# Later weight conversions for the second layer, token factors formed step by step, and a reordered last unit

## The chip, the cores and the metric

The kernel runs on one core of a Trainium2 chip. The metric is the device time of one execution in microseconds (us). TensorE (PE) multiplies, VectorE (DVE), ScalarE (ACT) and GpSimd (POOL) do the elementwise work, and SyncE (SP) and ACT issue DMA transfers. Each engine works through its own instructions in a fixed order and waits on semaphores for the others.

## The reference

Four batches of 576 tokens pass through three blocks:

```
phi(x)  = [exp(p), exp(-p)],  p = x w_phi - max|x w_phi|
attn    = phi(q) (phi(k)^T v) / (phi(q) sum_s phi(k) + 1e-6)
x       = heads of attn side by side                        # 4 x 576 x 512
u       = x + Re(FFT over tokens and features of x)
layer 1 : u + relu(norm(u) w_ch1) w_ch2                     # 512 -> 2048 -> 512
layer 2 : u = x + (relu(x^T w_tok1) w_tok2)^T               # tokens 576 -> 256 -> 576
          u + relu(u w_ch1) w_ch2                           # 512 -> 1536 -> 512
```

The weights of both layers come as 64-bit floats.

## The kernel before

All products are made in pairs of a rounded part ("high") and what is left ("low"): three matmuls (high-high, high-low, low-high) stand for one product. A weight must first be converted from its 64-bit words. `words` and `words2` do this for a block of 128x512: a DMA of 512 KB into a tile `raw`, one ACT instruction (L510), three DVE instructions on 128x512 words (L513, L514, L516). What follows splits the result into high (a copy on ACT) and low (a subtraction on POOL).

Layer 1's weights are converted by `w_ahead` (during the attention, stored to DRAM) and `w_now` (16 blocks for its third and fourth groups of hidden features, while its first groups are multiplied). Layer 2's channel weights go through `w_seven` and `wa_seven`: 24 blocks, in which four sums and differences of sub-blocks are made on POOL (L623 to L626), seven 128x128 parts are split (L632 on ACT, L636 on POOL), and high and low are stored to DRAM by SP (L645). Each of these 24 results is half of a tile `ring` of 1792 KB that `w_load` fetches later. Nine more blocks (`wa_plain`) hold the token weights.

Layer 2's channel products use seven products in place of eight, as in Strassen's scheme in Winograd's form. One `unit` takes 256 hidden features and one batch: seven products of token factors `x` with weights (`prod`, L859), sums and ReLUs on DVE, ACT and POOL that give seven new factors `g` (`part`, splits on POOL at L895, shown in the trace as L1283), and seven products of those (`prod2`, L868), each added to `u` on DVE by `flush` (L922, or L917 in the last unit of a batch, whose result goes to a tile `t` of three buffers and from there to DRAM). There are 24 units: batches 2 and 3 by turns through six parts of the features, then batches 0 and 1. The token factors of a batch (seven tiles `x`, from four differences `xq`) are made by `x_prep`: L827 on ACT, L830 on DVE or POOL, L833 on DVE.

The order on each engine is written out by a planner: every step is put on a list with a planned time (`at`, `later`), and the list is emitted in the order of these times. A planned time sets only the order; on the chip each instruction runs when its inputs and its place are there. Pools of tiles (`cv`, `cv2`, `r`, `g` and others) have fixed numbers of buffers, and a new tile waits for the last use of the buffer that it takes. Layer 1 ends where the token step (`c_tr`, `c_tok1`, `c_tok2`) begins.

In the traced execution: attention and FFT until about 320 us, layer 1 until 725, the token step until 790, the units until the end.

Of the kernel before, what the change touches and what calls it, by code (L numbers as in the profile page):

```python
# [9 lines left out]
F32 = mybir.dt.float32  # L10
# [36 lines left out]
HB = 288  # L47
# [7 lines left out]
def mixer_kernel(ctx: ExitStack, tc: tile.TileContext, qT, kT, vt, wphi, w11, w12, wt1, wt2, w21, w22,  # L55
# [439 lines left out]
    def words(src, n, cols, then, lag=0.0, tag="t"):  # L495

        home = P["cv2" if n is None or tag == "t2" else "cv"]
        raw = home.tile([128, 512, 2], U32, tag="raw", name="raw", bufs=2)
        if n is None:
            n = 128  # L500
            nc.sync.dma_start(out=raw.rearrange("q (j c) t -> q j c t", j=2), in_=src)
        else:
            nc.sync.dma_start(out=raw[0:n, 0:cols], in_=src)
        later(lag, words2, home, raw, n, cols, then, tag)

    def words2(home, raw, n, cols, then, tag):
        lo, hi = raw[0:n, 0:cols, 0], raw[0:n, 0:cols, 1]
        t = home.tile([128, 512], U32, tag=tag, name="t", bufs=2 if tag == "t2" else 1)
        v = t[0:n, 0:cols]
# [9 lines left out]
        later(V('dT', 2.8), then, v.bitcast(F32), *((raw,) if tag == 't2' else ()))  # L519
# [69 lines left out]
    def part_tile():  # L589
        return P["cv2"].tile([128, 7, 128], F32R, tag="y", name="wst", bufs=4)  # L590

    def wa_plain(key, src, n, cols):

        def then(v, raw):
# [19 lines left out]
    def wa_seven(key, src, eng):  # L614

        _, m, which, p, s = key

        def then(v, raw):
            blk = v.rearrange("q (a c) -> q a c", a=4)
            a11, a21, a12, a22 = (blk[:, n] for n in range(4))  # L620
            x = raw.rearrange("q c t -> q (c t)").bitcast(F32)[:, 0:512].rearrange("q (a c) -> q a c", a=4)
            ve = nc.gpsimd if eng == "pool" else nc.vector
            ve.tensor_tensor(out=x[:, 0], in0=a21, in1=a22, op=ALU.add)  # L623
            ve.tensor_tensor(out=x[:, 1], in0=x[:, 0], in1=a11, op=ALU.subtract)
            ve.tensor_tensor(out=x[:, 2], in0=a11, in1=a21, op=ALU.subtract)
            ve.tensor_tensor(out=x[:, 3], in0=a12, in1=x[:, 1], op=ALU.subtract)  # L626
            parts = [(slice(0, 1), blk[:, 0:1]), (slice(1, 3), blk[:, 2:4]), (slice(3, 7), x)]
            yh, yl = part_tile(), part_tile()

            def hi():  # L630
                for o, a in parts:
                    nc.scalar.copy(out=yh[:, o], in_=a)  # L632

            def lo():
                for o, a in parts:
                    nc.gpsimd.tensor_tensor(out=yl[:, o], in0=a, in1=yh[:, o], op=ALU.subtract)  # L636
                mark("wa", key)
                store(0, yh)

            def store(h, y):  # L640
                need(("wa", key))
                mark("wd", key)
                if (m, which, p) not in WD:
                    WD[m, which, p] = dr.tile([128, 2, 2, 7, 128], F32, name=f"wd{m}{which}{p}")
                nc.sync.dma_start(out=WD[m, which, p][:, s, h], in_=y.bitcast(F32))  # L645
            later(1.9, hi)
            later(3.2, lo)
            later(5.8, store, 1, yl)
        words(src, None, 512, then, V('wl', 5.0), 't2')

    def w_seven(p, which, s, eng="pool"):
# [161 lines left out]


    XI = {1: 0, 2: 1, 3: 2, 5: 3, 7: 4, 6: 5, 4: 6}
    WI = {1: 0, 2: 1, 4: 2, 5: 3, 6: 4, 7: 5, 3: 6}

    def x_prep(b, slot):

# [6 lines left out]
        def hi(n, a):  # L826
            nc.scalar.copy(out=X[n][:, 0], in_=a)  # L827

# [513 lines left out]
```

## Time and profile before

| | |
|---|---|
| median of 3 runs | 1104.27 us (1102.8 to 1104.54) |
| the profiled execution | 1102.2 us, of which its span is 1100.2 us |
| PE busy, matmuls | 1041.6 us, 7596 |
| DVE, ACT, POOL busy | 724.3, 447.5, 457.1 us |
| mean granted clock of PE | 0.98 |

Times in the rows are from the start of the span. A row of the stages gives the length of a stretch and, for each engine, its busy time with the number of instructions. Busy time of PE says little where its matmuls are held up, so the number of matmuls in a stretch is the better measure of pace.

### The profile page before, as it was taken

Reading aid. Unit: us, or ns where it says so; the run is one execution under the profiler, and the core shown is the slowest. Engines: PE = TensorE matmul, PEld = TensorE weight load, DVE = VectorE, ACT = ScalarE, POOL = GpSimd, SP = SyncE. Lnnn points to the kernel's source line nnn. Section 1 sums busy time; section 2 is a strip of 40 time slices with the busy share of each in tenths; the row PEclk is TensorE's granted clock in tenths of the full one; section 3 lists DMA queues with packets and bytes.
Section 4 is the critical chain, followed back from the end, with each engine's and each line's share of the span. In section 5 each row is a group of like instructions: output and inputs, shape, how many; then the busy total and the mean of one; then the engine's idle time right before and its main releaser. Section 6 shows DMA issues by size and latency. Waiting matters only on the chain.

```text
span 1100.2 us, 19639 instructions
## 1 busy us (share of the span) xinstructions
PE 1041.6 (95%) x7596; PEld 959.1 (87%) x7596; DVE 724.3 (66%) x1273; ACT 447.5 (41%) x1002; POOL 457.1 (42%) x483
## 2 busy tenths in 40 slices
PE   9999999999998788999998999999999998799997
PEld 9887787868898777999998999997889997799997
DVE  5788797999757788554466434246656667666665
ACT  6766556552124443332243212124344444434442
POOL 3363434322026654463444100001156657655654
PEclk9999999999999999999998999999999998899998
DMA  5565564362358764268643255450013543454532
GB/s 182 175 214 170 164 223 160 117 225 72 121 186 277 283 230 145 103 195 310 255 162 112 81 210 197 129 202 1 1 68 142 193 142 131 156 195 141 192 139 86
DMA packets 59945, 178.41 MB, mean 162 GB/s; under 512 B 7892, under 2 KB 23188, under 8 KB 53196
## 3 DMA queue, kind: packets, MB, share of 16 engines
q1 hardware_dynamic: 48332, 99.56, 27.4%
q10 hardware_dynamic: 11520, 77.60, 18.9%
q8 instruction: 60, 0.98, 0.4%
q14 instruction: 33, 0.27, 0.1%
HBM read 126.39 MB, written 48.31 MB: 159 GB/s over the span
## 4 chain that ended last, share of the span: by engine, by line
PE 52%; DVE 7%; POOL 3%; issue 2%; DMA 2%; ACT 1%; ACTq 0%; SPq 0%; DVEq 0%; POOLq 0%
PE pw L780 13%; PE pz L868 11%; PE pw L859 10%; PE pk L802 2%; PE pk L803 2%; PE pa L802 2%; PE pk L804 2%; PE pa L804 2%; PE pa L803 2%; DMA outT<-t 1%; POOL g L1283 1%; DVE t L514 1%; DVE xq L833 1%; PE pw L1062 1%; PE pk L1043 1%
## 5 line engine op out<-in xcount | busy, mean ns | idle before, releaser
L780 PE MATMUL pw<-xh,w 128*128 128x288 f32 x896 | 198.6, 296 | 0.0
L868 PE MATMUL pz<-g,ring 128*128 128x288 f32 x1008 | 160.5, 304 | 9.3 <-POOL g L1283 5.6
L859 PE MATMUL pw<-x,ring 128*128 128x288 f32 x1008 | 152.8, 298 | 8.6 <-DVE f L881 5.0
L788 DVE SCALAR_TENSOR_TENSOR gl<-pw,gh 128x288 fp32r<-128x288 f32 x128 | 57.9, 454 | 155.0 <-ACT gh L787 154.9
L868 PEld LDWEIGHTS pz<-g,ring 128*128 128x128 f32 x1008 | 143.8, 193 | 16.0 <-POOL g L1283 11.1
L922 DVE TENSOR_TENSOR u<-u,pz 128x576 f32<-128x576 f32 x152 | 114.3, 753 | 61.8 <-PE pz L868 58.0
L780 PEld LDWEIGHTS pw<-xh,w 128*128 128x128 f32 x896 | 151.2, 189 | 1.2 <-issue 1.0
L859 PEld LDWEIGHTS pw<-x,ring 128*128 128x128 f32 x1008 | 140.5, 190 | 11.4 <-DVE f L881 6.5
L780 PE MATMUL pw<-xl,w 128*128 128x288 f32 x448 | 133.0, 297 | 0.5 <-POOL xl L763 0.5
L787 ACT ACTIVATE gh<-pw 128x288 fp32r<-128x288 f32 x128 | 52.4, 409 | 195.3 <-PE pw L780 192.7
L1283 POOL TENSOR_TENSOR g<-t,g 128x576 fp32r<-128x576 f32 x48 | 70.6, 1470 | 54.4 <-ACT g L894 51.9
L199 POOL TENSOR_TENSOR l<-raw,h 128x384 fp32r<-128x384 f32 x48 | 51.7, 1081 | 95.3 <-ACT h L195 86.7
L803 PE MATMUL pk<-gl,w 128*128 128x288 f32 x256 | 78.9, 308 | 12.0 <-DVE gl L788 11.8
L802 PE MATMUL pk<-gh,w 128*128 128x288 f32 x256 | 77.6, 303 | 11.5 <-DVE u L807 5.1
L780 PEld LDWEIGHTS pw<-xl,w 128*128 128x128 f32 x448 | 84.8, 189 | 0.7 <-POOL xl L763 0.7
L1283 POOL TENSOR_TENSOR g<-f,g 128x288 fp32r<-128x288 f32 x72 | 59.3, 837 | 50.3 <-ACT g L894 50.3
L802 PE MATMUL pa<-gh,w 128*128 128x288 f32 x256 | 77.2, 302 | 0.0
L804 PE MATMUL pk<-gh,w 128*128 128x288 f32 x256 | 77.0, 301 | 0.0
L804 PE MATMUL pa<-gh,w 128*128 128x288 f32 x256 | 76.9, 300 | 0.0
L803 PE MATMUL pa<-gl,w 128*128 128x288 f32 x256 | 76.7, 299 | 0.0
L1283 ACT ACTIVATE f<-f 128x288 f32<-128x288 f32 x72 | 32.0, 444 | 101.8 <-DVE f L881 101.7
L259 PEld LDWEIGHTS pk<-v,ek 128*128 128x128 f32 x512 | 61.6, 192 | 5.8 <-issue 5.8
(195 smaller groups left out, 2400.7 us busy)
## 6 DMA issues: line engine op xcount, KB each, us to landing
ring<-wd ACTq DMA_DIRECT2D x24, 1792.0 KB
raw<-in_w SPq DMA_DIRECT2D x56, 512.0 KB
w<-wd ACTq DMA_DIRECT2D x24, 1024.0 KB
wd<-wst SPq DMA_DIRECT2D x48, 448.0 KB
wd<-wst SPq DMA_DIRECT2D x16, 512.0 KB
wd<-w ACTq DMA_DIRECT2D x32, 256.0 KB
v<-in_v SPq DMA_DIRECT2D x8, 650.0 KB
raw<-in_k SPq DMA_DIRECT2D x24, 192.0 KB
```

Of the source, the lines that this page charges most:

```text
L199: nc.gpsimd.tensor_tensor(out=l, in0=src, in1=h, op=ALU.subtract)
L259: nc.tensor.matmul(T["kv", i][j][:, o:o + 65], e[:, (t % 2) * 2 + j, s, :], v[:, t - 1, j * 65:j * 65 + 65], start=False, stop=(u == 1 and ...
L780: nc.tensor.matmul(out, w[:, k, fs], x[:, k, :], start=(n == 0), stop=(n == 11))
L787: nc.scalar.activation(out=gh, in_=out, func=AF.Relu)
L788: nc.vector.scalar_tensor_tensor(out=gl, in0=out, scalar=0.0, in1=gh, op0=ALU.max, op1=ALU.subtract)
L802: nc.tensor.matmul(out, wh[:, f % 4, ds], gh, start=(f == f0), stop=False)
L803: nc.tensor.matmul(out, wh[:, f % 4, ds], gl, start=False, stop=False)
L804: nc.tensor.matmul(out, wl[:, f % 4, ds], gh, start=False, stop=last)
L859: nc.tensor.matmul(out, w[:, kk, hw, WI[i]], x[XI[i]][:, hx, kk], start=(start and k == 0), stop=(stop and k == 5), skip_group_check=(i != 2))
L868: nc.tensor.matmul(o[s], w[:, s, hw, WI[i]], g[hx], start=(start and k == 0), stop=(stop and k == 2), skip_group_check=(i != 2))
L922: nc.vector.tensor_tensor(out=u, in0=u, in1=o, op=ALU.add)
L1283: fn(*a, **k)
```

## The change

- `w_seven` and `wa_seven` become one function. The seven parts are laid out so that one ACT copy and one POOL subtraction of 128x896 take the place of three each; the low half is written into `raw`, which has three buffers now; the load of a block is three DMAs instead of one.
- The 33 conversions for layer 2 begin 40 planned us before the end of layer 1's first three blocks (`tb2 - 40`), and not 20 after the FFT (`zend + 20`). Six of the 24 blocks (`late`) are left out there and converted from `td - 16` on, one each 15 planned us, `td` being the start of the units. These use the pool `cv`, whose tag `raw` the token step also uses.
- `ring` is loaded by SP and not by ACT.
- `x_prep` makes each token factor by itself: a high part is put just behind the old factor's last product, its low part 1.6 us later. For batches 2 and 3 all differences and low parts go to POOL; for batches 0 and 1 the differences go to DVE, and they begin three units and one unit earlier.
- In the last unit (`end`) the second products stand earlier and in another order, four splits and one sum move from POOL to DVE, and product 2 is flushed in two halves.

```diff
     def words(src, n, cols, then, lag=0.0, tag="t"):
-        home = P["cv2" if n is None or tag == "t2" else "cv"]
-        raw = home.tile([128, 512, 2], U32, tag="raw", name="raw", bufs=2)
+        home = P["cv2" if tag == "t2" else "cv"]
+        raw = home.tile([128, 512, 2], U32, tag="raw", name="raw", bufs=3 if tag == "t2" else 2)
...
     def part_tile():
-        return P["cv2"].tile([128, 7, 128], F32R, tag="y", name="wst", bufs=4)
+        return P["cv2"].tile([128, 7, 128], F32R, tag="y", name="wst", bufs=3)
...
-    def w_seven(p, which, s, eng="pool"):
+    def w_seven(p, which, s, late=False):
...
+        home = P["cv" if late else "cv2"]
+        raw = home.tile([128, 512, 2], U32, tag="raw", name="raw", bufs=2 if late else 3)
+        for o, n, j, c in ((0, 128, 0, 0), (128, 256, 1, 0), (384, 128, 0, 128)):
+            nc.sync.dma_start(out=raw[:, o:o + n], in_=src[:, j, c:c + n])
+        L = raw.rearrange("q c t -> q (c t)").bitcast(F32)[:, 0:896]
...
+        def then(v):
+            a11, a12, a22, a21 = (v[:, n * 128:(n + 1) * 128] for n in range(4))
+            x = [N["x"][:, n * 128:(n + 1) * 128] for n in range(4)]
+            for o, a, c, op in ((0, a21, a22, ALU.add), (1, x[0], a11, ALU.subtract), (2, a11, a21, ALU.subtract),
+                                (3, a12, x[1], ALU.subtract)):
+                nc.gpsimd.tensor_tensor(out=x[o], in0=a, in1=c, op=op)
...
+            def hi():
+                for o, e, a in N["parts"]:
+                    nc.scalar.copy(out=yh[:, o:e], in_=a)
+            def lo():
+                for o, e, a in N["parts"]:
+                    nc.gpsimd.tensor_tensor(out=L[:, o:e], in0=a, in1=yh[:, o:e].bitcast(F32), op=ALU.subtract)
+                store(0, yh.bitcast(F32))
...
+            later(V('sh', 3.2), hi)
+            later(V('sl', 4.8), lo)
+            later(V('ss', 8.0), store, 1, L)
+        later(12.0 if late else V('wl', 5.0), words2, raw, room, then)
...
     def w_load(which, p, v):
-        nc.scalar.dma_start(out=t.bitcast(F32), in_=WD[1, which, p])
+        nc.sync.dma_start(out=t.bitcast(F32), in_=WD[1, which, p])
...
+    XP = {1: 2, 0: 1, 5: 6, 4: 7, 3: 5, 2: 3, 6: 4}
+    POS = {2: 0, 1: 1, 6: 4, 7: 5, 5: 8, 3: 11, 4: 13}
+    def x_prep(b, slot, td_, t0, step, engs):
...
         def diff(o, a, c):
-            nc.vector.tensor_tensor(out=o, in0=a, in1=c, op=ALU.subtract)
+            (nc.gpsimd if "d" in engs else nc.vector).tensor_tensor(out=S_[o], in0=S_[a], in1=S_[c], op=ALU.subtract)
...
+        for n, a in enumerate(((3, "12", 0), (5, 2, 3), (4, 2, "12"), (6, 1, 5))):
+            at(td_ + 0.01 + step * n, diff, *a)
+        for n, i in XP.items():
+            t = t0(POS[i])
+            at(t, hi, n)
+            at(t + 1.6, lo, n)
...
         def y2():
-            open_z("y")
-            second(2, "y", True, True, 0, 0)
+            if not end:
+                open_z("y")
+                return second(2, "y", True, True, 0, 0)
+            o = [pw()[:, 0:HB] for _ in range(2)]
+            prod2(2, o, True, True)
+            for m in range(2):
+                later(0.3, flush, o[m].unsqueeze(1), 0, 0, (m,))
...
-        for k, fn in ((20, x1), (21, z7), (23, x6), (24, z4), (26, x5), (30, y2), (31, x3)):
+        second_ = ((20, x1), (21, z7), (23, x6), (24, z4), (26, x5), (30, y2), (31, x3))
+        if end:
+            second_ = ((17.1, x1), (17.6, z7), (18.2, x6), (18.8, x5), (19.2, x3), (19.8, y2), (20.4, z4))
+        for k, fn in second_:
             at(t0 + k * st_, fn)
...
-    tcv = zend + V('c2', 20)
+    late = ahead[18:24]
+    del ahead[18:24]
+    tcv = tb2 - V('c2', 40)
     for n, (kind, *a) in enumerate(ahead):
         at(tcv, w_seven if kind == "s" else wa_plain, *a)
-        tcv += V('c3', 12) if n < 8 else V('c4', 9.3)
+        tcv += V('c4', 9.3)
...
-    at(td - 36, x_prep, 2, 0)
-    at(td - 20, x_prep, 3, 1)
-    at(times1[11] - 0.6, x_prep, 0, 0)
-    at(times1[12] - 0.6, x_prep, 1, 1)
+    x_prep(2, 0, td - 44, lambda k: td - 42.5 + 1.4 * k, 1.6, "d0123456")
+    x_prep(3, 1, td - 22, lambda k: td - 21 + 1.6 * k, 1.6, "d0123456")
+    x_prep(0, 0, times1[8], lambda k: times1[10] + (k + 8) * TU / 14, TU / 3, "016")
+    x_prep(1, 1, times1[11] + 11 * TU / 14, lambda k: times1[11] + (k + 9) * TU / 14, 0.7, "016")
+    for n, (_, p, which, s) in enumerate(late):
+        at(td - 16 + 15 * n, w_seven, p, which, s, True)
```

On POOL, in a unit of the channel products, the order before is (L902 and L909 make sums for the factors, L1283 splits them):

```order
L902 TENSOR_TENSOR t<-f 128x288
L1283 TENSOR_TENSOR g<-t,g 128x576
L909 TENSOR_TENSOR t<-f,t 128x288
L1283 TENSOR_TENSOR g<-f,g 128x288 x2
L1283 TENSOR_TENSOR g<-t,g 128x576
L1283 TENSOR_TENSOR g<-f,g 128x288
```

In the changed kernel POOL meets this in one of the first units (L919 and L926 are the old L902 and L909, L1319 the old L1283; L644 and L656 belong to a late conversion):

```order
L926 TENSOR_TENSOR t<-f,t 128x288
L1319 TENSOR_TENSOR g<-f,g 128x288 x2
L644 TENSOR_TENSOR raw<-t 128x128
L644 TENSOR_TENSOR raw<-raw,t 128x128
L644 TENSOR_TENSOR raw<-t 128x128
L644 TENSOR_TENSOR raw<-t,raw 128x128
L1319 TENSOR_TENSOR g<-t,g 128x576
L656 TENSOR_TENSOR raw<-raw,wst 128x512
L656 TENSOR_TENSOR raw<-t,wst 128x384
L1319 TENSOR_TENSOR g<-f,g 128x288
```

A block of four small instructions now stands ahead of the unit's last split of 128x576, and a block of two larger ones behind it. Six conversions bring two such blocks each; in the units their places differ.

On DVE, where the units turn from batches 2 and 3 to batches 0 and 1, the order before is (L833 makes a difference, L830 a low part of a token factor, L881 and L922 belong to units):

```order
L833 TENSOR_TENSOR xq<-u 128x576
L881 TENSOR_TENSOR f<-pw,c_10526 128x288
L833 TENSOR_TENSOR xq<-u,xq 128x576
L881 TENSOR_TENSOR f<-pw,c_10629 128x288
L833 TENSOR_TENSOR xq<-u 128x576
L922 TENSOR_TENSOR u<-u,pz 128x2x288
L833 TENSOR_TENSOR xq<-u,xq 128x576
L922 TENSOR_TENSOR u<-u,pz 128x2x288
L830 TENSOR_TENSOR x<-xq,x 128x576 x2
L922 TENSOR_TENSOR u<-u,pz 128x2x288
L830 TENSOR_TENSOR x<-xq,x 128x576
```

For the same batch DVE has this in the changed kernel (L845 is the old L833, L898 the old L881, L940 the old L922):

```order
L845 TENSOR_TENSOR xq<-u 128x576
L898 TENSOR_TENSOR f<-pw,c_10149 128x288
L940 TENSOR_TENSOR u<-u,pz 128x2x288 x2
L845 TENSOR_TENSOR xq<-u,xq 128x576
L940 TENSOR_TENSOR u<-u,pz 128x2x288 x2
L898 TENSOR_TENSOR f<-pw,c_10205 128x288
L845 TENSOR_TENSOR xq<-u 128x576
L940 TENSOR_TENSOR u<-u,pz 128x2x288 x2
L920 TENSOR_TENSOR t<-f 128x288
```

The differences stand three units earlier and further apart, and the low parts follow in later units.

The end of DVE's order before is this (L917 writes an output tile `t`):

```order
L881 TENSOR_TENSOR f<-pw,c_12381 128x288
L917 TENSOR_TENSOR t<-u,pz 128x576 x2
L922 TENSOR_TENSOR u_8405<-u_8405,pz 128x2x288 x3
L917 TENSOR_TENSOR t<-u_8405,pz 128x576 x4
```

Now it is this (L935 is the old L917; the L1319 are splits that were on POOL):

```order
L898 TENSOR_TENSOR f<-pw,c_12321 128x288
L1319 TENSOR_TENSOR g<-t,g 128x576
L926 TENSOR_TENSOR t<-f,t 128x288
L1319 TENSOR_TENSOR g<-t,g 128x288
L1319 TENSOR_TENSOR g<-f,g 128x288
L935 TENSOR_TENSOR t<-u,pz 128x576
L1319 TENSOR_TENSOR g<-t,g 128x288
L935 TENSOR_TENSOR t<-u,pz 128x576
L940 TENSOR_TENSOR u_8222<-u_8222,pz 128x2x288 x3
L935 TENSOR_TENSOR t<-u_8222,pz 128x576 x2
L935 TENSOR_TENSOR t<-u_8222,pw 128x288 x2
L935 TENSOR_TENSOR t<-u_8222,pz 128x576
```

Five instructions stand ahead of the flushes that the last unit's first second products wait for, and five output tiles follow one another where there were four.

## Rows read from the trace of the kernel before

**Rows 1.** The page: PE's busy time, and its granted clock in tenths, 40 slices.

```profile
PE 1041.6 (95%) x7596; PEld 959.1 (87%) x7596; DVE 724.3 (66%) x1273; ACT 447.5 (41%) x1002; POOL 457.1 (42%) x483
...
PEclk9999999999999999999998999999999998899998
```

**Rows 2.** Stages: length, busy time and count by engine, clock, DMA share, GB/s.

```profile
320.00:430.00 110.00, 88.61 (x576) 83.33 (x576) 87.72 (x134) 44.79 (x95) 64.82 (x78) 0.94 0.71 243
...
570.00:600.00 30.00, 25.97 (x177) 25.53 (x176) 19.67 (x33) 9.72 (x21) 16.58 (x22) 0.89 0.28 102
600.00:720.00 120.00, 120.00 (x905) 120.00 (x904) 45.29 (x107) 24.22 (x59) 11.94 (x13) 1.00 0.42 145
...
905.00:985.00 80.00, 67.80 (x454) 64.56 (x454) 54.44 (x82) 35.07 (x80) 51.58 (x44) 0.91 0.41 145
985.00:1085.00 100.00, 99.80 (x734) 97.48 (x733) 63.82 (x104) 42.51 (x102) 60.90 (x62) 1.00 0.41 151
```

**Rows 3.** DVE's groups in 320 to 430 us: count, busy us, mean ns, idle before.

```profile
L516 DVE SCALAR_TENSOR_TENSOR t<-raw,t 128x512 uint32<-128x512 uint32 x23 | 21.1, 916 | 0.8
L514 DVE SCALAR_TENSOR_TENSOR t<-raw,t 128x512 uint32<-128x512 uint32 x23 | 19.7, 855 | 0.8
L513 DVE TENSOR_SCALAR t<-t 128x512 uint32<-128x512 uint32 x23 | 15.9, 693 | 6.7 <-ACT t L510 4.3 <-POOL w L537 2.1 <-POOL wst L636 0.3
```

**Rows 4.** Tile wst in 320 to 430 us: min/median/max ns, first and last start.

```profile
L632 ACT CAST wst<-raw x8: 613/620/622, 330.2 to 419.9; 128x512 fp32r<-128x512 f32 x8
```

**Rows 5.** Timeline of DVE, 390 to 394 us: start, duration, instruction.

```profile
391.79 1.66 DVE L514 SCALAR_TENSOR_TENSOR t<-raw,t 128x512 uint32<-128x512 uint32 x1
393.49 0.69 DVE L516 SCALAR_TENSOR_TENSOR t<-raw,t 128x512 uint32<-128x512 uint32 x1
```

**Rows 6.** PE's waits in 570 to 600 us: total, times, longest.

```profile
PE pk L802 <- ACT wst L632: 3.9, 1, 3.9
```

**Rows 7.** PE's waits in 720 to 795 us, and groups of ACT and DVE there.

```profile
PE pk L1043 <- DVE ytl L1029: 3.2, 2, 1.9
...
L1028 ACT CAST yth<-pw 128x512 fp32r<-128x512 f32 x16 | 9.1, 587 | 19.0 <-PE pw L1022 19.0
...
L1029 DVE TENSOR_TENSOR ytl<-pw,yth 128x512 fp32r<-128x512 f32 x16 | 10.7, 683 | 9.7 <-ACT yth L1028 9.7
```

**Rows 8.** PE's waits in 905 to 985 us.

```profile
PE pz L868 <- POOL g L1283: 4.9, 4, 2.0
```

**Rows 9.** Timeline of DVE, 916 to 925 us.

```profile
916.87 1.99 DVE L833 TENSOR_TENSOR xq<-u 128x576 f32<-128x576 f32 x1
...
919.15 0.74 DVE L833 TENSOR_TENSOR xq<-u,xq 128x576 f32<-128x576 f32 x1
```

**Rows 10.** The chain of waits, 905 to 985 us: start, length, what.

```profile
959.90 8.31 DMA outT<-t
```

**Rows 11.** Timeline of POOL and of PE's weight loads, one unit from 1048 us; idle in brackets.

```profile
1051.78 1.43 POOL L1283 TENSOR_TENSOR g<-t,g 128x576 fp32r<-128x576 f32 x1 [2.15 <-ACT g L894]
...
1055.47 1.44 POOL L1283 TENSOR_TENSOR g<-t,g 128x576 fp32r<-128x576 f32 x1
...
1056.96 1.48 PEld L868 LDWEIGHTS pz<-g,ring 128*128 128x128 f32 x11 [0.26 <-POOL g L1283]
...
1058.42 0.81 POOL L1283 TENSOR_TENSOR g<-f,g 128x288 fp32r<-128x288 f32 x1 [1.51 <-ACT g L894]
...
1060.00 1.08 POOL L902 TENSOR_TENSOR t<-f 128x288 f32<-128x288 f32 x1 [0.77 <-ACT f L885]
```

**Rows 12.** Two short stretches: a ring load lands in the first, a conversion's DMAs in the second.

```profile
1053.60:1060.00 6.40, 6.38 (x49) 6.14 (x48) 3.52 (x7) 2.61 (x7) 4.12 (x5) 1.00 0.78 288
566.00:572.00 6.00, 6.00 (x48) 6.00 (x47) 4.72 (x8) 1.24 (x4) 0.32 (x1) 1.00 0.69 240
```

**Rows 13.** The chain of waits at the end.

```profile
1094.25 1.86 DMA outT<-t
...
1096.23 0.75 DVE t L917
```

More of the change, by code (lines that the diff above doesn't have):

```diff
@@ L495, in words, with room, words2 @@
     def words(src, n, cols, then, lag=0.0, tag="t"):
[L497 to L509 removed]
+        home = P["cv2" if tag == "t2" else "cv"]
+        raw = home.tile([128, 512, 2], U32, tag="raw", name="raw", bufs=3 if tag == "t2" else 2)
+        nc.sync.dma_start(out=raw[0:n, 0:cols], in_=src)
+        def room():
+            if tag == "t2":
+                return home.tile([128, 1024], U32, tag=tag, name="t", bufs=2)[0:n, 0:cols]
+            return home.tile([128, 512], U32, tag=tag, name="t", bufs=1)[0:n, 0:cols]
+        later(lag, words2, raw[0:n, 0:cols], room, then)
+    def words2(raw, room, then):
+        lo, hi, v = raw[:, :, 0], raw[:, :, 1], room()
         nc.scalar.activation(out=v.bitcast(F32), in_=hi.bitcast(F32), func=AF.Abs, scale=2.0 ** -112)
@@ L518, in words2 @@
         later(V('dB', 0.8), bits)
-        later(V('dT', 2.8), then, v.bitcast(F32), *((raw,) if tag == 't2' else ()))
+        later(V('dT', 2.8), then, v.bitcast(F32))
     def w_src(m, g, which, k):
@@ L612, in wa_plain @@
         words(src, n, cols, then, V('wl', 5.0), 't2')
[L614 to L649, printed above, removed]
-    def w_seven(p, which, s, eng="pool"):
+    def w_seven(p, which, s, late=False):
         a = (w21, w22)[which]
@@ L850, in unit @@
+    def unit(p, b, v, last, t0, tu, end=False):
         st_ = tu / 14
@@ L894, in part @@
             nc.scalar.copy(out=ga[:, 0], in_=src)
-            later(0.6, nc.gpsimd.tensor_tensor, out=ga[:, 1], in0=src, in1=ga[:, 0], op=ALU.subtract)
+            later(0.6, (nc.vector if end else nc.gpsimd).tensor_tensor, out=ga[:, 1], in0=src, in1=ga[:, 0], op=ALU.subtract)
         def one(i, key):
@@ L951, in s_x3 @@
             later(1.0, sums1)
-            later(2.8, lambda: part((5, 7), h["t13"], 2))
+            later(2.2 if end else 2.8, lambda: part((5, 7), h["t13"], 2))
+            if end:
+                later(2.7, lambda: part(6, h["t24"][:, 0:1]))
         def s_z4():
@@ L956, in s_z4 @@
             later(0.3, lambda: relu("21", h["Z"], h["c2"]))
+            if end:
+                later(1.4, sums2)
+                later(1.5, one, 2, "21")
+                later(2.2, lambda: part(4, h["t24"][:, 1:2]))
+                return
             later(2.0, one, 2, "21")
```

88 lines of the change are left out of this document (51 added, 37 removed).

## The prediction

> **What bounds the kernel now.** I read the page first: PE is busy for 95% of the span and its granted clock dips in a few slices [rows 1]. So a gain must come from stretches in which PE is held up. The views by stage show them when matmuls are counted and not busy time. Where nothing disturbs layer 1, PE makes 905 matmuls in 120 us, 7.54 per us; in undisturbed units it makes 734 in 100 us, 7.34 per us, which is 11.45 us for a unit's 84 [rows 2]. By these paces 320 to 430 us holds 576 / 7.54 = 76.4 us of work in 110, so 33.6 us are lost. 570 to 600 holds 177 / 7.54 = 23.5 us, 6.5 lost. 905 to 985, where the units turn to batches 0 and 1, holds 454 / 7.34 = 61.9 us, 18.1 lost. These losses include the clock: its mean there is 0.94, 0.89 and 0.91, which mixes 1.2 and 2.4 GHz, while in the two undisturbed stretches it is 1.00 [rows 2].
>
> Then I read what PE waits for. In the first stretch DVE is busy for 87.7 of 110 us, more than in any other of these stages [rows 2], and 23 conversions take 21.1 + 19.7 + 15.9 = 56.7 us of that, 2.47 each [rows 3]. Eight of the 23 belong to layer 2 [rows 4]. At 570 us one wait of 3.9 us stands for most of the loss [rows 6]. At the turn PE waits for splits on POOL, up to 2.0 us at a time [rows 8], and DVE works off `x_prep` in between [rows 9].
>
> **The change, part by part.** All terms are set against the profiled execution, 1102.2 us with a span of 1100.2. The median is 1104.27, so 2.1 us are added at the end.
>
> *Conversions leave the first stretch.* The planned start moves behind the stretch, so the eight conversions and their POOL sums and splits go. DVE loses 8 x 2.47 = 19.7 us. The other 15 may become shorter too: L514 takes 1.66 us in one place, L516 of the same shape 0.69 right behind it, against means of 0.86 and 0.92 [rows 3, 5]. At 0.69 for both, 15 x 0.39 = 5.9 us would go; I take half. DVE then has 87.7 - 19.7 - 3 = 65 us of work. Bounds: if DVE stays as full as it was (80%), the stretch takes 81 us, a gain of 29. If PE's loss falls only with the number of conversions, 8/23 of 33.6, it is 12. I take 23, nearer to the first, because DVE is the engine that is full there. What is late next is layer 1's own conversion and its normalisation, which share DVE.
>
> The Trainium skill (SBUF — State Buffer, "SBUF: two separate sides") says that GpSimd and a VectorE instruction with two operands in SBUF lock one port pair against each other for the whole instruction. The 1.66 against 0.69 us agrees with it. By this rule alone the full 5.9 us would go with the POOL work, and the term would be some 3 us larger; POOL keeps layer 1's splits, so I do not take it.
>
> *27 conversions behind it.* They follow one another every 9.3 planned us, as those in that stretch did. There PE ran at full pace but for the wait at 580 us [rows 6]. The new places miss that coincidence or make another. Bounds: all 6.5 us gone, or one more wait of 3.9; I take -3. Three load DMAs in place of one, and one wide copy and split for three, I cost at nothing: they lie beside that full pace. Without this cover a longer split would hold DVE a little more, as above.
>
> *Token step.* DVE no longer makes differences for `x_prep` there; POOL does, which is idle then. PE's 3.2 us of waiting for `ytl` go [rows 7], and about 1 us of slow clock behind them. But the first late conversion takes one of the two `raw` buffers in the middle of the last batch, so that its last three transposed tiles share the other. Each then waits for the products of the one before, and PE for 0.59 us on ACT and 0.68 on DVE [rows 7], partly under transposes: 1 us each, 3 in all. Sum -1; bounds -5 (no such wait) and +4.
>
> *Six conversions beside the units.* Each puts four small instructions (128 columns; between 0.36, by the columns of a 1.43 us split of 576, and 0.81, the time of 288) and one split of 896 columns (2.2 us by the same rate) on POOL, about 2.0 and 2.2 us [rows 11]. In a unit POOL is free for 2.15 + 1.51 + 0.77 = 4.4 us, in three pieces [rows 11]. PE waits 0.26 us for the last 576-column split, which ends at 1056.91, so that one has no slack at all [rows 11]. By the order on POOL four of the blocks stand where they delay it: each costs PE about 2 us, 8 in all. DVE's 2.47 us [rows 3] per conversion I put at 0.5 on the path, since DVE is busy for only 64% there [rows 2]: 3 in all. I take +11. Bounds: +4 (most blocks fall into gaps) and +20 (a whole split and half of DVE's share on the path, 6 x 3.4).
>
> *The turn.* The 18.1 us come from work that stood between PE's products. The same work now lies ahead of need: per batch eight DVE instructions at 0.74 (1.99 where it collides) [rows 9], three splits on POOL and seven copies on ACT, over some five units in which DVE has 4 us free each [rows 2]. Not all of it will fit, and the output tiles still wait for their DMA, 8.3 us in one place [rows 10]. I expect 6 us to stay lost: -12. Bounds -16 and -5.
>
> *Ring loads on SP.* ACT is freed of 0.4 us each and not held up; nothing on the path changes as long as a load is early. I cost it at 0; the price if it is not is a rival below.
>
> *The last unit.* Its second products can start earlier, but DVE now has five instructions more ahead of the flush that frees their accumulator, and five output tiles in three buffers. Before, the last flush waited for the DMA of the tile three before, 1.86 us, and started at 1096.23 [rows 13]. Now the tile three before is the flush of product 3, itself among the last: its DMA (1.9 us and 0.4 to issue) and a flush of 0.75 follow one another, about 3 us, and PE's better order gives back about 2. I take +1, bounds -4 and +4.
>
> Sum: -23 - 3 - 1 + 11 - 12 + 1 = -27. 1102.2 - 27 = 1075, and with 2.1 to the median 1077 us.
>
> **The rivals.**
>
> *More of everything.* The first stretch follows DVE's share (-29), the wait at 580 us goes (-6.5), token step -3, units +5, turn -16, end -1: -50, 1054 us. For it: PE's losses are all waits for engines that get less to do. Against it: twelve blocks on POOL with no slack behind one split.
>
> *DVE still sets the pace of the first stretch.* Only -12 there, and the same engine pushes the late ones to +16; the rest as above: -11, 1093 us. For it: 65 us of DVE work beside 76 us of PE work, in fixed order with normalisations.
>
> *Ring loads come late.* SP's one queue now carries a ring load (6.4 us at 288 GB/s), a conversion's loads and stores (about 1.4 MB, 6 us at 240 GB/s) and later the output [rows 12]. Per unit this is 6.4 + 6 x 11.45 / 15 = 11 us of 11.45. A load that stands behind a conversion is up to 5 us late; at three changes of weights, with part of it hidden, some 10 us, and 4 more where outputs stand behind a load at the turn: 1091 us. Against it: three buffers, and SP issues in the planned order.
>
> The Trainium skill (DMA: Bandwidth & Descriptors, "Queues, rings and completion order") says that descriptors of one issuing engine's ring are consumed in order, while different rings take turns. That speaks against putting both on SP. The 8.31 us of the output DMA [rows 10] were measured with ring loads in another ring, so this trace does not show it.
>
> *Slower.* The place is POOL and DVE in the first six units: if each late conversion costs PE its whole 4.2 us on POOL and 2.47 on DVE, 6.7 us, that is +40 against -38 from all else: +2, 1106 us. It decides from 6.3 us per conversion. For it: fixed order and a split without slack. Against it: 4.4 us of gaps per unit.
>
> **How the numbers follow.** Forecast 0.52 (its own range 1066 to 1088), more of everything 0.14, DVE in the first stretch 0.18, late ring loads 0.10, slower 0.06. The range 1056 to 1094 leaves out half of the second case, the upper end of the third and fourth, and the last: just under 0.2. No change means within 0.2%, 2.2 us, about what a measurement of this kernel can tell. Four of the five cases are faster by more than that, with small tails: faster 0.92, same 0.02, slower 0.06.
>
> **What would show it.** Right: 320 to 400 us holds close to 576 matmuls and DVE is below 70 us there; no wait of PE for `c` or `x` at the turn; PE waits for POOL splits in units 1 to 6, about 2 us at four or five places; three short waits for `yth` or `ytl` at the end of the token step; the last flush waits for an output DMA. Wrong: PE's wait for ring loads in the units, or DVE still 80% busy and PE short of 7 matmuls per us in the first stretch.

## The result and the profile after

The changed kernel takes 1084.51 us (median of 4 runs, 1082.92 to 1085.0), the kernel before, run beside it, 1104.16 (1102.8 to 1104.54). The ratio is 0.9822, 95% interval 0.9805 to 0.9839: 19.7 us faster, where 27 were forecast. Its profiled span is 1083.3 us, 16.9 shorter than before's.

The page, PE's busy time and granted clock (answers to [rows 1]):

```profile
PE 1030.6 (95%) x7596; PEld 951.3 (88%) x7596; DVE 711.2 (66%) x1265; ACT 442.2 (41%) x961; POOL 460.1 (42%) x451
...
PEclk9999999999999999999999999999999999999999
```

The same matmuls in 11 us less busy time, with no dip left that shows in tenths. Where the time went is seen by stage, with the columns of [rows 2]:

```profile
320.00:400.00 80.00, 76.29 (x550) 74.66 (x549) 59.35 (x103) 31.31 (x61) 25.18 (x20) 0.98 0.59 201
320.00:430.00 110.00, 105.79 (x770) 103.95 (x769) 80.43 (x142) 40.78 (x78) 40.37 (x36) 0.98 0.52 177
...
528.00:560.00 32.00, 30.37 (x229) 30.17 (x228) 25.69 (x42) 11.22 (x20) 15.15 (x18) 1.00 0.45 161
...
768.00:886.00 118.00, 100.69 (x713) 96.51 (x712) 77.25 (x119) 52.26 (x125) 84.42 (x92) 0.99 0.48 174
...
890.00:960.00 70.00, 62.43 (x442) 60.42 (x442) 49.91 (x75) 34.43 (x77) 47.62 (x43) 0.98 0.49 178
```

I divide the counts by the prediction's paces, 7.54 per us in layer 1 and 7.34 in the units. In 320 to 430 us 770 matmuls are 102.1 us of work, so 7.9 are lost where 33.6 were. In 528 to 560, where the wait of [rows 6] stood, 1.6 are lost and not 6.5. The turn, now in 890 to 960, loses 70 - 442 / 7.34 = 9.8 and not 18.1. The units ahead of it have got worse: 768 to 886 loses 118 - 713 / 7.34 = 20.9 us. Before, the stretch that begins at the same place:

```profile
797.00:905.00 108.00, 105.16 (x770) 102.45 (x770) 65.69 (x108) 46.96 (x113) 65.56 (x66) 1.00 0.37 137
```

There it was 108 - 770 / 7.34 = 3.1. So the units beside the six late conversions lose 17.8 us more; what of this is theirs, the experiments show.

DVE's groups in 320 to 430 us after (answers to [rows 3]):

```profile
L515 DVE SCALAR_TENSOR_TENSOR t<-raw,t 128x512 uint32<-128x512 uint32 x17 | 12.7, 749 | 0.6
L513 DVE SCALAR_TENSOR_TENSOR t<-raw,t 128x512 uint32<-128x512 uint32 x17 | 11.8, 692 | 0.6
L512 DVE TENSOR_SCALAR t<-t 128x512 uint32<-128x512 uint32 x17 | 10.4, 610 | 0.9 <-ACT t L509 0.9
```

A conversion takes 2.05 us of DVE and not 2.47. PE's waits in the units with late conversions, 755 to 886 us:

```profile
PE pz L885 <- POOL g L1319: 7.7, 6, 2.9
PE pz L885 <- DVE u L940: 4.9, 3, 1.9
PE pw L876 <- DVE f L898: 3.4, 4, 1.4
PE pw L876 <- ACT c L891: 1.8, 3, 1.2
```

17.8 us of waits, of which those for POOL's splits are less than half. The longest, until 783.68 us, is read in POOL's timeline: the four sums (L644) of a late conversion, the first of which is shown, stand ahead of the 576-column split (L1319) for which PE waits, and the conversion's own split (L656) follows.

```profile
780.47 0.44 POOL L644 TENSOR_TENSOR raw<-t 128x128 f32<-128x128 f32 x1
...
782.23 1.40 POOL L1319 TENSOR_TENSOR g<-t,g 128x576 fp32r<-128x576 f32 x1
783.59 1.28 POOL L656 TENSOR_TENSOR raw<-raw,wst 128x512 f32<-128x512 f32 x1
```

The longest wait for a flush, 1.9 us until 836.18, is read on DVE: the flush (L940) that frees the accumulator stands behind a late conversion's instructions (L513, L515), and these take 1.80 and 1.17 us here.

```profile
832.46 1.80 DVE L513 SCALAR_TENSOR_TENSOR t<-raw,t 128x512 uint32<-128x512 uint32 x1
834.30 1.17 DVE L515 SCALAR_TENSOR_TENSOR t<-raw,t 128x512 uint32<-128x512 uint32 x1
835.38 1.41 DVE L940 TENSOR_TENSOR u<-u,pz 128x576 f32<-128x576 f32 x2
```

PE's waits at the turn, 885 to 965 us (answers to [rows 8]):

```profile
PE pw L876 <- DMA ring<-wd: 2.9, 1, 2.9
PE pz L885 <- POOL g L1319: 2.1, 2, 1.4
PE pw L876 <- DVE f L898: 2.0, 1, 2.0
```

With one more of 0.5 us these are 7.5 us. The granted clock is 0.79 in 922 to 930 us, which costs 8 x 0.21 = 1.7 us more: 9.2 of the 9.8 that the turn loses.

The end, in the chain of waits (answers to [rows 13]):

```profile
1062.92 1.85 DMA outT<-t
...
1077.19 1.87 DMA outT<-t
```

There are now two waits for an output tile's DMA here. PE waits for the flushes:

```profile
PE pz L885 <- DVE t L935: 3.3, 2, 2.4
PE pz L885 <- DVE u L940: 0.8, 1, 0.8
```

### The profile page after: what moved, and what is told of

Its sections match the earlier page's. It is cut to its first block, busy times and chain, and to the rows that moved or that the text cites. A ratio compares the mean times of both kernels' runs of the same rounds, so it can differ in the third digit from the quotient of the medians.

```text
span 1083.3 us, 19688 instructions
## 1 busy us (share of the span) xinstructions
PE 1030.6 (95%) x7596; PEld 951.3 (88%) x7596; DVE 711.2 (66%) x1265; ACT 442.2 (41%) x961; POOL 460.1 (42%) x451
## 4 chain that ended last, share of the span: by engine, by line
PE 56%; DVE 9%; POOL 5%; issue 3%; ACT 1%; DMA 1%; ACTq 0%; DVEq 0%; POOLq 0%
PE pw L790 16%; PE pz L885 9%; PE pw L876 8%; POOL g L1319 3%; PE pk L813 3%; PE pk L812 3%; PE pk L814 3%; PE pa L812 3%; PE pa L814 3%; PE pa L813 3%; PE pw L1094 1%; PE pa L1094 1%; DVE t L513 1%; PE pk L1075 1%; DVE t L512 1%
## 5 line engine op out<-in xcount | busy, mean ns | idle before, releaser
L885 PE MATMUL pz<-g,ring 128*128 128x288 f32 x1002 | 157.6, 301 | 19.5 <-POOL g L1319 9.8
L885 PEld LDWEIGHTS pz<-g,ring 128*128 128x128 f32 x1002 | 141.4, 191 | 25.9 <-POOL g L1319 14.5
L940 DVE TENSOR_TENSOR u<-u,pz 128x576 f32<-128x576 f32 x152 | 113.9, 752 | 56.4 <-PE pz L885 52.9
L1319 POOL TENSOR_TENSOR g<-t,g 128x576 fp32r<-128x576 f32 x46 | 66.3, 1442 | 52.4 <-ACT g L911 49.6
L812 PE MATMUL pk<-gh,w 128*128 128x288 f32 x256 | 76.4, 298 | 4.7 <-ACT gh L797 2.8
L812 PE MATMUL pa<-gh,w 128*128 128x288 f32 x256 | 75.9, 297 | 0.0
L814 PE MATMUL pk<-gh,w 128*128 128x288 f32 x256 | 75.8, 296 | 0.0
L814 PE MATMUL pa<-gh,w 128*128 128x288 f32 x256 | 75.6, 295 | 0.0
L1319 ACT ACTIVATE f<-f 128x288 f32<-128x288 f32 x72 | 32.0, 444 | 90.3 <-DVE f L898 90.1
L1319 POOL TENSOR_TENSOR g<-f,g 128x288 fp32r<-128x288 f32 x69 | 58.1, 856 | 20.4 <-ACT g L911 20.2
```

Of the source, the lines that this page charges most:

```text
L812: nc.tensor.matmul(out, wh[:, f % 4, ds], gh, start=(f == f0), stop=False)
L814: nc.tensor.matmul(out, wl[:, f % 4, ds], gh, start=False, stop=last)
L885: nc.tensor.matmul(o[s], w[:, s, hw, WI[i]], g[hx], start=(start and k == 0), stop=(stop and k == 2), skip_group_check=(i != 2))
L940: nc.vector.tensor_tensor(out=u, in0=u, in1=o, op=ALU.add)
L1319: fn(*a, **k)
```

## The experiments

All edits are to the changed kernel unless said otherwise. Each run's ratio is against the kernel before on its own chip; differences from the changed kernel are differences of these ratios times 1104 us.

**The first stretch.** The early start is put back:

```diff
-    tcv = tb2 - V('c2', 40)
+    tcv = zend + V('c2', 20)
...
-        tcv += V('c4', 9.3)
+        tcv += V('c3', 12) if n < 8 else V('c4', 9.3)
```

> The changed kernel with the 27 conversions started where the kernel before starts them, 92 planned us earlier, eight of them 12 us apart. Theory (DVE's conversions hold up PE in the first stretch): 20 to 26 us come back between 320 and 430 us: 1104 to 1110 us. Rival (the first stretch gained because the conversions are built differently: POOL makes the four sums, one wide split in place of three, no sums on POOL reading the raw tile): the time stays below 1095 us.

1107.74 us, ratio 1.0042 (1.0022 to 1.0061): 24 us slower than the changed kernel. The second run keeps the early start and leaves out DVE's part:

```diff
-        later(V('dB', 0.8), bits)
-        later(V('dT', 2.8), then, v.bitcast(F32))
+        if not skip:
+            later(V('dB', 0.8), bits)
+        later(V('dT', 2.8), then, v.bitcast(F32))
```

> The kernel with the 27 conversions started early again (1107.7 us), which leaves out DVE's three instructions in all conversions behind layer 1's (weights of layer 2 and of the token step are wrong); loads, copies, POOL's work and stores stay. Theory (DVE set the pace of the first stretch): of the 25 us that came back between 320 and 430 us, 18 to 25 go again, 1083 to 1090 us. Rival (the loads and stores, 246 GB/s there, or POOL's sums and splits held PE up): 1098 us or more.

1082.42 us, ratio 0.9816 (0.9795 to 0.9836). The first stretch of the two, with the early start, and then with the early start and without DVE's part:

```profile
320.00:430.00 110.00, 89.68 (x580) 84.25 (x579) 89.71 (x135) 43.10 (x78) 63.23 (x60) 0.92 0.71 246
```

```profile
320.00:430.00 110.00, 101.12 (x702) 96.93 (x701) 78.48 (x124) 48.50 (x88) 70.31 (x71) 0.97 0.76 264
```

The early start holds 580 matmuls, nearly the 576 of before [rows 2], though its conversions are built in the new way, so the way they are built is not what gained. Against the changed kernel 190 are missing, 25.2 us. Without DVE's part 122 of them are back, 16.2 us, less than the 18 I expected at least: DVE's instructions are two thirds of the term. The rest stays with what else a conversion does there (POOL, ACT, transfers), which no run took apart. The total came back in full for another reason: that run also frees the late conversions of DVE's part, and by the starts of the same instructions it gained 8.7 us on the changed kernel there.

**No late conversion.**

```diff
-    late = ahead[18:24]
-    del ahead[18:24]
+    late = []
...
-        tcv += V('c4', 9.3)
+        tcv += V('c4', 7.55)
...
-        later(12.0 if late else V('wl', 5.0), words2, raw, room, then)
+        later(12.0 if late else 9.0, words2, raw, room, then)
```

> The changed kernel with no conversion beside the units: all 24 of layer 2 and the 9 others are made before the token step, one every 7.55 planned us in place of 9.3, with a shorter planned lead of the loads (9.0 for 14.6). Theory (the six late conversions cost the units 18 us, the step from a lead of 28.8 us at unit 0 to 10.9 at unit 9): about 18 us less in the units, and up to 4 us more in layer 1, where 33 conversions now stand closer: 1067 to 1071 us. Rival (the units lose their 18 us to something else that came with the change, the ring loads on SP or the earlier turn): 1080 to 1085 us, and PE's waits for splits in units 0 to 9 stay near 8 us. Second rival (what is taken from the units is paid in layer 1, where DVE works off the conversions): 1080 us or more with new PE waits between 400 and 650 us.

All 24 are made before the token step now, closer together and with a shorter lead of the loads. 1072.7 us, ratio 0.971 (0.9689 to 0.9732): 12.4 us gained. Its units and PE's waits in them, 755 to 886 us:

```profile
768.00:886.00 118.00, 114.28 (x834) 111.09 (x834) 72.84 (x124) 49.91 (x121) 68.62 (x69) 1.00 0.36 129
```

```profile
PE pw L876 <- DVE f L898: 2.5, 3, 1.3
PE pz L885 <- POOL g L1318: 1.0, 2, 0.7
```

834 matmuls are 113.6 us: 4.4 lost and not 20.9, so 16.5 us are the late conversions'. With the 4.7 us of the token step (below) that is 21.2. About half of it is paid in layer 1, more than the 4 us I allowed: by the start of the same instruction this kernel is 0.5 us behind at 327 us and 11.4 behind when layer 1 ends. PE has three new long waits there, until 398.15, 542.45 and 580.16 us. The first and the last read alike. DVE and POOL ahead of the last, of 2.9 us, for the L817 that is shown:

```profile
576.08 2.48 DVE L513 SCALAR_TENSOR_TENSOR t<-raw,t 128x512 uint32<-128x512 uint32 x1
578.59 0.69 DVE L515 SCALAR_TENSOR_TENSOR t<-raw,t 128x512 uint32<-128x512 uint32 x1
...
579.57 0.81 DVE L817 TENSOR_TENSOR u<-u,pk 128x288 f32<-128x288 f32 x2
```

```profile
575.71 2.30 POOL L656 TENSOR_TENSOR raw<-t,wst 128x896 f32<-128x896 f32 x1
```

L513, which takes 0.69 us when nothing holds it, as L515 does here, has taken 2.48: POOL's split ends at 578.01, and DVE's instruction 0.55 us behind it. At 389.77 us it is an L512 that takes 2.50 us in place of 0.43, beside a split of layer 1 of 1152 columns. The wait until 542.45 goes back to a raw tile's DMA that landed at 537.62.

**Which engine makes the late ones dear.** Three runs take parts of the six late conversions away. POOL's part:

```diff
-                nc.gpsimd.tensor_tensor(out=x[o], in0=a, in1=c, op=op)
+                if not late:
+                    nc.gpsimd.tensor_tensor(out=x[o], in0=a, in1=c, op=op)
...
-                for o, e, a in N["parts"]:
+                for o, e, a in N["parts"] if not late else ():
```

> The changed kernel whose six late conversions make no sums and no splits on POOL (it leaves these out and stores the copies twice, so weights of units 8 to 11 are not the reference's); their loads, DVE's three instructions and ACT's copies stay. With no late conversion the units were 18 us shorter and the end of the token step 5. Theory (POOL's order is the price, in the forecast's proportion of 8 on POOL to 3 on DVE): 13 us of the units' 18 go, 1069 to 1073 us. Rival (DVE is the price: its three instructions stand ahead of work that frees PE's accumulators): 4 us go, 1079 to 1082 us.

The loads and ACT's copies stay, and the high half is stored in the low half's place too. DVE's part (`words2` called with `skip` for the late ones, as above):

> The changed kernel whose six late conversions leave out DVE's three instructions (the sign and the low word are not put in, so weights of units 8 to 11 are wrong); POOL's and ACT's work stays. Theory (POOL's order is the price): 4 to 5 us of 18 go, 1079 to 1081 us. Rival (DVE is the price): 13 us go, 1070 to 1073 us. If both this and the run without POOL's work gain more than 13 us, the price is the meeting of the two engines and not the work of either.

Both parts:

> The changed kernel whose six late conversions leave out both POOL's sums and splits and DVE's three instructions (weights of units 8 to 11 are wrong); their loads, ACT's pass and copies and their stores stay. From the token step's end to unit 10, having no late conversion at all gained 22 us, leaving out POOL's part 6, DVE's part 7. Theory (the two parts add up, and some 9 us are the tiles, ACT's copies and transfers): 13 us, 1070 to 1073 us. Rival (either part is hidden where the other one holds the same product up, so that the two together are worth nearly all): 18 to 21 us, 1064 to 1067 us. Second rival (both are worth what one is): 7 us, 1077 us.

Measured: 0.9788 (0.9767 to 0.9809) without POOL's, 3.8 us gained; 0.977 (0.9747 to 0.9792) without DVE's, 5.7; 0.9692 (0.9655 to 0.9728) without both, 14.4. The units, and PE's two largest waits in 755 to 886 us, without POOL's part:

```profile
768.00:886.00 118.00, 107.45 (x752) 103.61 (x753) 80.36 (x125) 53.65 (x128) 67.08 (x65) 0.97 0.53 190
```

```profile
PE pz L886 <- DVE u L941: 4.9, 3, 1.9
PE pw L877 <- DVE f L899: 3.2, 4, 1.3
```

Without DVE's part:

```profile
768.00:886.00 118.00, 107.38 (x759) 104.33 (x760) 68.99 (x113) 53.34 (x126) 86.45 (x97) 0.97 0.52 186
```

```profile
PE pz L886 <- POOL g L1320: 7.1, 6, 2.5
PE pw L877 <- DVE f L899: 3.1, 4, 1.4
```

Without both:

```profile
768.00:886.00 118.00, 113.61 (x827) 110.19 (x827) 72.45 (x120) 60.48 (x143) 70.64 (x71) 1.00 0.57 206
```

Neither engine is the price alone. All of PE's waits in the units' products there come to 17.8 us in the changed kernel, 11.1 without POOL's part, 11.6 without DVE's, 4.3 without both and 3.5 with no late conversion at all. So POOL's part is 6.7 us of waits and DVE's 6.2, and they add up, nearly: 13.5 for both. Without DVE's part the waits for flushes (L940, 4.9 us) are gone; those for L898, a sum that reads another accumulator, are 3.4 us in the changed kernel and 2.5 with no late conversion, so they are hardly the conversions'. In time the parts do not add up: by the counts the lost time is 20.9, 15.5, 14.6, 5.3 and 4.4 us, so one part is worth 5.4 or 6.3 and both 15.6. The clock fits the difference. Its mean is 0.97 in the runs with one part left, which have two stretches at 1.2 GHz there, 0.99 in the changed kernel, which has one, and 1.00 without both. In 118 us a mean of 0.97 costs 3.5 us and one of 0.99 costs 1.2; waits and clock together are then 19.0, 14.6, 15.1, 4.3 and 3.5 us, within 2 of the lost time in each run. This is one trace of each. In the medians the parts are 3.8 and 5.7 against 14.4 for both, each 2 to 4 us either way, which does not settle it. The first theory, that the parts add up to 13, was right on the waits and by the traces too low on the time.

**The last late load and the token step.** All six begin 9 planned us later:

```diff
-        at(td - 16 + 15 * n, w_seven, p, which, s, True)
+        at(td - 7 + 15 * n, w_seven, p, which, s, True)
```

> The changed kernel with all six late conversions begun 9 planned us later, so that the first takes its raw tile behind the last of the token step's transposed tiles. Theory (the shared tile costs 3 us at the end of the token step, the four waits of 0.7 to 1.1 us): these waits go; the units cost what they cost, 1080 to 1082 us. Rival (the waits at the end of the token step belong to the step and not to the shared tile): still there, 1084 us. Second rival (the place of the six against the units matters most): the units change by more than 4 us either way.

1085.7 us, ratio 0.9837 (0.9815 to 0.9859), the same as the changed kernel and not the 1080 to 1082 expected. The waits at the end of the token step, 735 to 766 us, were these:

```profile
PE pk L1074 <- ACT yth L1060: 1.1, 3, 0.7
PE pk L1075 <- DVE ytl L1061: 0.7, 3, 0.2
```

They are gone, while without POOL's part and without both parts, where the load stays, they are the same: the shared tile is their cause. From the end of layer 1 to the first product of the units the step takes 4.7 us less, 3.2 of them by its last product of `yth`; the rest falls behind it, where the changed kernel's clock is 0.76 in 755 to 759 us and this one's 1.00. The units gave back 6.1 us. PE's waits there, in the new places:

```profile
PE pz L885 <- POOL g L1319: 12.0, 8, 2.7
PE pw L876 <- DVE f L898: 5.1, 5, 2.5
```

With 2.1 us of others these are 19.2 us and not 17.8, and the clock in 768 to 886 us is 0.94 and not 0.99. So the place of the six against the units changes them by more than 4 us, as the second rival had it, but by less than their presence.

**The turn.** The ring loads go back to ACT, and in another run the three splits of `x` that each batch has on POOL at the turn go to DVE:

```diff
-        nc.sync.dma_start(out=t.bitcast(F32), in_=WD[1, which, p])
+        nc.scalar.dma_start(out=t.bitcast(F32), in_=WD[1, which, p])
```

> The changed kernel with the ring loads issued by ACT again. Theory (the load's place on SP matters once: PE waits 2.9 us for a ring load at 946 us, all else is early): 1080 to 1083 us, that wait gone. Rival (the wait is for the buffer that becomes free late, and not for the queue): 1084 us, the wait still there. Second rival (ACT, which must wait in order for a free buffer, now holds up copies for the units): 1087 us or more.

```diff
-    x_prep(0, 0, times1[8], lambda k: times1[10] + (k + 8) * TU / 14, TU / 3, "016")
-    x_prep(1, 1, times1[11] + 11 * TU / 14, lambda k: times1[11] + (k + 9) * TU / 14, 0.7, "016")
+    x_prep(0, 0, times1[8], lambda k: times1[10] + (k + 8) * TU / 14, TU / 3, "")
+    x_prep(1, 1, times1[11] + 11 * TU / 14, lambda k: times1[11] + (k + 9) * TU / 14, 0.7, "")
```

> The changed kernel with all seven splits of batches 0 and 1 at the turn on DVE, in place of four there and three on POOL. Theory (part of the 9 us still lost at the turn is POOL's: two splits of 1.4 us stand at 901.5 ahead of the splits for which PE waits at 912.8): 2 to 3 us gained, 1082 us. Rival (DVE, which already holds up products there with 2.0 us, is the engine that is late): 2 to 5 us lost, 1086 to 1090 us. Second rival (the turn is bound by the output's stores and the ring load behind them): no change.

With the loads on ACT: 1083.24 us, ratio 0.9808 (0.9791 to 0.9824), no difference that can be told. The load at the turn is issued at 936.08 and not at 940.77 us, 4.7 us earlier, of which 1.8 are the lead that this run has there anyway. PE's wait for it falls to 0.9 us:

```profile
PE pw L876 <- DMA ring<-wd: 0.9, 1, 0.9
```

By the starts of the same instructions it gained nothing over the turn: its lead of 1.3 us stems from before 326 us, is 1.8 ahead of the turn and 1.9 behind it. At the load itself it was 3.5 us; a unit later, 0.3 us of waiting for DVE and 0.7 for a split on POOL, which the changed kernel does not have there, stand in the place of the wait that went. With the three splits on DVE: 1087.12 us, 0.9848 (0.9832 to 0.9863); it is 1.2 us behind before the turn, by a stretch at 1.2 GHz at 812 us, ahead of what the edit moves, and 1.2 behind after it; 1.3 more are lost at the end. Both left the turn at its 9 us. Which of its waits would give time back if it went was not found; that the output's DMAs bound it, the second rival, was not tried by itself, and no run put the old `x_prep` back.

**The last unit.** The old order:

```diff
-        unit(p, b, v, p == ps[-1], times1[n], TU, n == len(order1) - 1)
+        unit(p, b, v, p == ps[-1], times1[n], TU)
```

> The changed kernel with the last unit in the old order. Theory (the lead falls from 19.7 us at unit 16 to 16.9 at the end, so the new order costs 2.7 us): 1081 to 1083 us. Rival (forecast: +1): 1083.5 us. Second rival (the new order gains, and the loss at the end comes from the DMA of the output tiles alone, whatever the order): 1085 to 1088 us.

1082.89 us, ratio 0.9814 (0.9788 to 0.984), which the medians cannot tell from the changed kernel. The traces can: 0.2 us behind at the flush at 1055 us, 2.5 ahead at the end of the span, 2.7 for the old order. PE waits once for a flush there and not three times (and once, 0.9 us, for a split on POOL):

```profile
PE pz L885 <- DVE t L935: 2.1, 1, 2.1
```

**A version that beats both.** No late conversion, the old last unit, and POOL's split in four pieces of 224 columns (ACT's copy stays whole):

```diff
-            N["parts"] = [(0, 896, t.bitcast(F32)[:, 0:896])]
+            N["wide"] = [(0, 896, t.bitcast(F32)[:, 0:896])]
+            N["parts"] = [(o, o + 224, t.bitcast(F32)[:, o:o + 224]) for o in range(0, 896, 224)]
```

> The kernel without late conversions (1072.7 us), with POOL's split of 896 columns made in four of 224, and the last unit in the old order. Theory (in that kernel three waits of PE of 2 to 3.4 us in layer 1 stand behind DVE instructions of 2.5 us in place of 0.43 to 0.70, each beside one POOL instruction of 2.3 to 2.7 us; the two are locked together as long as the one POOL instruction runs): no conversion instruction of DVE over 1.5 us beside these splits, 3 to 5 us gained there, 2 to 3 at the end: 1065 to 1068 us. Rival (what was late there are the raw tiles' DMAs or the closer places of the conversions): only the end's 2 to 3 us, 1070 us.

1067.02 us, ratio 0.9677 (0.9653 to 0.9701): 16 us below the changed kernel. DVE's two-operand instructions in layer 1 from 380 to 680 us, with the wide split (the run without late conversions) and with the narrow one:

```profile
L513 DVE SCALAR_TENSOR_TENSOR t<-raw,t 128x512 uint32<-128x512 uint32 x27 | 31.1, 1151 | 0.9
...
L515 DVE SCALAR_TENSOR_TENSOR t<-raw,t 128x512 uint32<-128x512 uint32 x27 | 21.9, 812 | 0.9
```

```profile
L513 DVE SCALAR_TENSOR_TENSOR t<-raw,t 128x512 uint32<-128x512 uint32 x27 | 26.7, 987 | 1.0
L515 DVE SCALAR_TENSOR_TENSOR t<-raw,t 128x512 uint32<-128x512 uint32 x27 | 24.7, 915 | 0.9
```

L513 got shorter and L515 longer: with the wide split 10 of the 54 took more than 0.75 us, seven of them over 2.4; with the narrow one 32 did, most of them 1.04 us. With L512, down from 22.2 to 16.7 us in all, DVE's three instructions fell from 75.2 to 68.1 us. PE's wait until 580 us is gone. This kernel is 8.0 us behind the changed one at the end of layer 1 and not 11.4, and the end gained 2.6. The same was then done to layer 1's own split of 1152 columns:

```diff
-            (nc.gpsimd if le == "pool" else nc.vector).tensor_tensor(out=l, in0=src, in1=h, op=ALU.subtract)
+            for k in range(4):
+                (nc.gpsimd if le == "pool" else nc.vector).tensor_tensor(out=l[:, k], in0=src[:, k], in1=h[:, k], op=ALU.subtract)
```

> The kernel without late conversions, with narrow splits and the old last unit (1067.0 us), in which layer 1's own split of 1152 columns (2.69 us on POOL) is made in four of 288 too. Theory (DVE's 2.50 us at 389.6 in place of 0.43, ahead of a wait of PE of 3.4 us, lasts as long as that one split): no DVE instruction of a conversion over 2 us near 390 us, 2 to 4 us gained, 1063 to 1065 us. Rival (that wait is due to how many DVE instructions stand there, two conversions and one normalisation): the time stays at 1067 us. Second rival (four instructions in place of one make each split later): 1069 us or more.

1067.74 us, ratio 0.9667 (0.9649 to 0.9685), the same. DVE near that place:

```profile
392.80 1.18 DVE L513 SCALAR_TENSOR_TENSOR t<-raw,t 128x512 uint32<-128x512 uint32 x1
394.01 1.18 DVE L515 SCALAR_TENSOR_TENSOR t<-raw,t 128x512 uint32<-128x512 uint32 x1
...
396.17 1.64 DVE L513 SCALAR_TENSOR_TENSOR t<-raw,t 128x512 uint32<-128x512 uint32 x1
```

No instruction takes 2.5 us any more, but several take a little more, and PE's wait stays, 3.6 us at 400 us. That fits the rival, two conversions in a row; but POOL's four pieces took 4.17 us where the one split took 2.67, so this run does not part the number of DVE's instructions from POOL's longer work. The same total hides two differences: by the starts of the same instructions this kernel is 2.6 us behind the one before at 339 us (1.9 of it from before 254 us, where runs of the same code differ by as much), and 0.8 ahead of it at the end of layer 1. So some 3 us were gained, behind the place that was aimed at.

## Why the prediction was right, and where its sizes were off

The direction, the places and the sign of every term were right; the sum was 7 us too good, and the six late conversions, taken for less than the turn, cost twice what it gave. Term by term, forecast and measured by stage:

| term | forecast | measured |
|---|---|---|
| first stretch | -23 | -25.7 |
| conversions behind it | -3 | -4.9 |
| token step | -1 | -0.7 |
| six late conversions, in the units | +11 | +17.8 |
| the turn | -12 | -8.3 |
| ring loads on SP | 0 | 0 |
| last unit | +1 | +2.7 |

These add up to -19.1, near the 19.7 of the medians; the spans differ by 16.9, and 1.2 of the 2.2 between lies ahead of 254 us, where the change touches nothing. That the sum came out no worse is in part luck: 4.6 us more than forecast in the first two terms hide as much of the 12.2 less in the late conversions, the turn and the last unit.

*First stretch.* DVE set its pace, as said, for two thirds of the term by the run without its part; that the instructions left would get shorter was taken by half, and came in full: 2.05 for 2.47 us per conversion. The rival by which DVE still sets the pace there (-12) is out. The sign I gave for 320 to 400 us, some 576 matmuls, was too much, since 550 stand there; but 770 by 430 us is more than the term needed, (110 - 33.6 + 23) x 7.54 = 749.

*Token step.* PE's waits of [rows 7] went, the shared `raw` tile brought short ones, six of 1.8 us in all, and the shift of the late loads shows whose they are and what they cost: 4.7 us where 3 were taken, with the slow clock behind them. The rest of the step gained 5.4 where 4 were taken, so the -0.7 is two errors that cancel; that the rest is `x_prep`'s, no run shows by itself.

*The six late conversions* are the step that was mis-sized. POOL's share, 8 forecast, is 6.7. (The 0.36 us forecast for an instruction of 128 columns is a slip, since 1.43 x 128 / 576 is 0.32; the sums took 0.45, and the block 1.8 us where 2.0 were forecast.) DVE's, "0.5 on the path" each because DVE is busy for 64%, is 1.0 each, 6.2: the flush that frees an accumulator stands behind 2 us and more of the conversion in DVE's order, and a mean share of 64% says nothing of that. The clock was left out: with the two parts 15.6 us went and not the 12.9 of their waits. What is left of the 16.5 us that went with no late conversion, 0.9, is ACT's and the transfers' share.

*The turn.* Waits for `c` or `x` are gone, as forecast; that this is `x_prep`'s doing is argued from the traces and was not tried. 9.8 us stay lost and not 6: 7.5 of waits for POOL, DVE and a DMA, and the clock. Two parts were tried without effect; which one binds is open.

*Ring loads.* One sign of being wrong came: PE waited 2.9 us for a ring load. The rival's mechanism was there, a load behind twelve output DMAs, and its price was not: with that load issued by ACT, 2 us of the wait went and nothing was gained.

*Last unit.* The sign was right and the size too small, 2.7 and not 1. Two waits for an output tile's DMA in place of one, and flushes late behind them: the mechanism was named, the order's return of 2 us did not come.

## What to carry to other kernels

Work that is moved beside a full engine costs by what stands behind it in each in-order queue and not by the mean share of that engine; ask of each queue which instruction frees the next product. Where two engines hold up the same product stream, taking away one can show less than its part, as here by the clock that fell again, so take away both in a run of its own. And compare stages by how much work they hold, since here a gain of 40 us and a loss of 20 lay in one total.

## What the runs showed of the hardware

A DVE instruction of a conversion that began while a POOL instruction ran ended a fixed time behind that one's end, whenever it had begun. In layer 1 of the run without late conversions all ten L513 and L515 of this kind ended 0.55 us behind it, and the sixteen L512, which read one tensor, that had more than 0.1 us of it ahead, 0.28 or 0.29. So an L513 took 2.48 us and not 0.69 beside a split of 896 columns (2.30 us), and an L512 2.50 us and not 0.43 at 389.6 us in the version with narrow splits, beside one of 1152 columns (2.67 us). The Trainium skill (SBUF — State Buffer, "SBUF: two separate sides") calls this an exclusive lock that is held for a whole instruction, for VectorE instructions with two inputs in SBUF (against a GpSimd instruction that reads SBUF) or in a two-port mode; the trace agrees for the two-input L513 and L515, and in which mode the L512 ran no run shows. So the width of POOL's instructions sets the longest stall of DVE, and narrow ones make more stalls of a shorter kind: with 224 columns L513 fell from 1.15 to 0.99 us in the mean and L515 rose from 0.81 to 0.92. They are not free on POOL: four took 4 x 0.815 = 3.3 us where one took 2.18. Part of that may be waiting, since the median piece took 0.675 us and the longest 1.79:

```profile
L657 POOL TENSOR_TENSOR raw<-t,wst 128x224 f32<-128x224 f32 x96 | 75.3, 815 | 32.6 <-ACT wst L653 31.5 <-DMA u<-sp 1.0
```

```profile
L656 POOL TENSOR_TENSOR raw<-t,wst 128x896 f32<-128x896 f32 x24 | 52.2, 2176 | 32.9 <-ACT wst L652 32.9
```
